# Pairing the PV matmuls behind a score tile in a statically scheduled attention and feed-forward kernel

## The chip, the cores and the metric

The kernel runs on one core of one Trainium2 chip. The metric is the device time of a run in microseconds. Next to the times I use positions read from the traces: when the first projection matmul starts, when the last matmul starts, and where TensorE waits in between.

## The reference, cut to what matters

```python
# x: 2048 tokens x 512; 32 heads of 16; four segments of 512 tokens
for s in range(4):
    logits = einsum(qs, ks) * scale + causal_mask
    a_dot  = einsum(softmax(logits), vs)                    # "score" and "PV"
    a_mem  = (phi(qs) @ M) / (phi(qs) @ z + 1e-6)           # memory numerator, denominator
    o      = sigmoid(beta) * a_mem + (1 - sigmoid(beta)) * a_dot
    M, z   = M + phi(ks).T @ vs, z + phi(ks).sum()
a = o @ wo
h = relu(x @ W_gate) * (x @ W_up);  b = h @ W_down
out = g * a + (1 - g) * b                                   # g = sigmoid(x . gate_w)
```

`phi(t)` is `t + 1` for positive t and `exp(t)` otherwise. On the chip it is an exponential on ACT, then a ramp and a minimum on DVE. TensorE does all the products, ACT the exponentials, POOL the causal mask of the score tiles, and DVE most reads of PSUM.

## The kernel before

The kernel contains a small list scheduler in Python. Every operation is given a planned duration. Before launch the scheduler simulates the five engines and fixes the order on each of them, and the semaphores that keep that order safe. **The order is static.** On the chip nothing is re-decided: if an operation takes longer than planned, whoever was placed behind it waits.

```python
class Sched:
    def _choose(self, e):               # which head of e's queues is placed next
        for q in self.queues[e]:
            ...
            rt = self.ready(op, e)      # planned time at which it could start
            if rt is not None:
                heads.append((q[0], rt, op))          # q[0] is the queue's priority
        ...
        rdy = [h for h in heads if h[1] <= now + 20.0]
        if rdy:
            best = min(rdy, key=lambda h: (h[0], h[1]))
            ...
```

Accumulators use four PSUM banks. A bank is free for a new matmul group when the group that held it has been read by DVE or ACT. Score tiles use the array as four 32-row tiles (mode "r"), PV as four 17-column tiles in 32-column strips (mode "c"), and everything else uses the whole array (mode "f"):

```python
# score tile: 4 heads side by side, one tile per 32 rows
q.matmul(PL[:, jj, o:o + w], lhsT=V.kp[32 * jj:32 * jj + 32, ...], rhs=V.qT[32 * jj:32 * jj + 32, ...],
         start=True, stop=True, tile_position=(32 * jj, 0), ...)
# mask of the diagonal block, on POOL
pool(lambda g, ap=ap: g.affine_select(out=ap, in_=ap, compare_op=ALU.is_ge, fill=0.0, base=0,
                                      pattern=[[0, 4], [1, 128]], channel_multiplier=-1), t_pool(512), ...)
# PV: two operations (p = 0, 1) per group of 8 heads, each with a bank of its own
q.matmul(A(ep)[32 * jj:32 * jj + 17, c:512], lhsT=V.vaug[...], rhs=V.E[:, e, jj, o:o + w],
         start=(j == 0), stop=(j == 3), tile_position=(0, 32 * jj), ...)
# order of one group:  score A0, score B0, [PV pair of the group before], score C, score A1, score B1
```

The argument later turns on two small DVE items. The first is 64 small copies (32 partitions, four gate values in each), which may go to DVE or ACT. In the code they are called `gexpT`. The second is the minimum that finishes phi of the queries, which the denominator matmuls ("den") read:

```python
gq["flex"].append(sc.add(Op([("dve", lambda e, ...: e.tensor_copy(dst, V.gexp[32 * a:32 * a + 32, t0:t1]), 150),   # planned ns
                             ("act", lambda e, ...: e.activation(dst, V.gexp[...], ACT.Copy), 215)], ..., name="gexpT")))
sbs.append(dve(lambda e, G=G: e.tensor_tensor(V.phiq[:, G, :], V.phiq[:, G, :], V.ttmp[:, G % 2, :], ALU.min), t_dve(512, 2), ...))
...
pes.append(pe(fden, 16 * 30, reads=[f"phiq{G}" for G in range(4)] + ["Mbd16"], name=f"den{s}", ep=ep, role="w"))
```

At the start TensorE runs five dummy matmuls until x arrives, transposes x, runs four more dummies, and begins the first projection. The dummies read a tile that DVE zeroes.

The softmax here doesn't subtract the row's maximum and nothing guards it: scores larger than these inputs give would overflow.

Of the kernel before, what the change touches and what calls it, by code (L numbers as in the profile page):

```python
# [13 lines left out]
LAT = 60.0  # L14
# [40 lines left out]

class Op:
    __slots__ = ("engs", "eng", "fns", "occs", "lat", "reads", "writes", "name", "dma", "nbytes", "mode", "ep", "role",
                 "after", "preds", "stream", "idx", "start", "end", "done", "cidx")

    def __init__(self, alts, reads=(), writes=(), name="", lat=0.0, dma=False, nbytes=0, mode="f", ep=None, role=None):  # L60
        self.engs = [a[0] for a in alts]
        self.fns = {a[0]: a[1] for a in alts}
        self.occs = {a[0]: float(a[2]) for a in alts}
        self.eng = self.engs[0] if len(alts) == 1 else None
        self.lat = lat
        self.reads = tuple(reads)
        self.writes = tuple(writes)
        self.name = name
        self.dma = dma
        self.nbytes = nbytes  # L70
        self.mode = mode
        self.ep = ep
        self.role = role
        self.after = 0.0
        self.preds = []
        self.stream = self.idx = self.start = self.end = None
        self.done = False
        if ep is not None:
            if role == "r":
                ep.readers.append(self)  # L80
                self.reads = self.reads + (ep.res,)
            else:
                self.writes = self.writes + (ep.res,)


class Sched:
# [75 lines left out]
    def queue(self, prio, ops):  # L162
# [4 lines left out]
        for e, ts in by.items():  # L167
            self.queues[e].append([prio, ts, 0])

    def _bank_choice(self, op, e):  # L170
        cls = op.ep.cls
        if cls != "att":
            held = 0
            nheld = 0
            for prev in self.bank_ep:
                if prev is None or all(r.done for r in prev.readers):
                    continue
                held += prev.cls == cls
                nheld += 1
            if held >= self.CAPS.get(cls, 2) or nheld >= len(self.bank_ep) - 1:  # L180
                return None
        best = None
        for bi, prev in enumerate(self.bank_ep):
            ft = 0.0
            if prev is not None:
                if not all(r.done for r in prev.readers):
                    continue
                for r in prev.readers:
                    if self.know[e][r.stream] < r.idx:
                        ft = max(ft, r.end + LAT)  # L190
            if best is None or ft < best[1]:
                best = (bi, ft)
        return best
# [7 lines left out]
    def ready(self, op, e):  # L201
        t0 = self.now[e]
        t = op.after
        for p in self._pred_done(op, e):
            if not p.done:
                return None
            if self.know[e][p.stream] < p.idx:
                t = max(t, p.end + LAT)
        if op.ep is not None:
            if op.role == "w" and op.ep.bank is None:  # L210
                for rd in op.ep.readers:
                    for p, _ in rd.preds:
                        if p.ep is op.ep or p.cidx > op.cidx:
                            continue
                        if not p.done:
                            return None
                        t = max(t, p.end - op.occs["pe"] - (3000.0 if op.ep.cls == "out" else 300.0))
                bc = self._bank_choice(op, e)
                if bc is None:
                    return None  # L220
                t = max(t, bc[1])
            elif op.ep.bank is None:
                return None
        if e == "pe" and t > 0:
            t += 80.0
        return max(t, t0)
# [59 lines left out]
    def _choose(self, e):  # L286
        heads = []
        for q in self.queues[e]:
# [4 lines left out]
            op = q[1][q[2]]  # L293
            rt = self.ready(op, e)
            if rt is not None:
                heads.append((q[0], rt, op))
        if not heads:
            return None
        now = self.now[e]
# [81 lines left out]
def program(sc, nc, T, PL, PA, A_x, A_wq, A_wk, A_wv, A_wo, A_beta, W_g, W_u, W_d, gate_w, out, NSEG, KT, NF, NT, EPS, SCALE):  # L381
# [23 lines left out]
    def A(ep):  # L405
        return PA[ep.bank]
# [10 lines left out]
        load(eng, [f"hT{i}"], V.hT[:, i, :], x0[:, i, :], 1 << 17)  # L417
    for nm, w, src in (("wq", V.wq, A_wq), ("wk", V.wk, A_wk), ("wv", V.wv, A_wv)):
        for kt in range(KT):
            load("act" if nm == "wq" and kt % 2 else "sp", [f"{nm}{kt}"], w[:, kt, :], src[kt * 128:(kt + 1) * 128, :], 1 << 17)  # L420
    load("act", ["g4"], V.g4[:], gate_w.rearrange("(kt p) -> kt p", p=128), 1 << 12)
    half = (NF // 2) * 128
    hs_ = ((0, half), (half, NF * 128))
# [46 lines left out]
    sc.queue(1, st)  # L470

    ds = []
    ds.append(dve(lambda e: e.memset(V.rl[:, 0, 0:128], 0.0), 130, writes=["rl0"], name="warm0"))
    for b in range(4):
        ds.append(dve(lambda e, b=b: e.memset(PA[b][:], 0.0), 500, writes=[f"init{b}"], name=f"init{b}"))
    ds.append(dve(lambda e: e.reduce_sum(V.pm[:, :], pm8, AX.X), 180, reads=["pm8"], writes=["pm"], name="pm"))
    sc.queue(0, ds)

    def warm(n, k, b):
        def fn(e):  # L480
            for i in range(n):
                ins = e.matmul(PL[:, b, :], lhsT=V.rl[:, 0, 0:128], rhs=V.rl[:, 0, 0:128].unsqueeze(1).to_broadcast([128, 4, 128]), start=True, stop=True)  # L482
            return ins
        return pe(fn, n * (427 if k == 0 else 260), reads=["rl0"], writes=[f"bankL{b}"], name=f"warm{k}")

    xps, xcs = [warm(5, 0, 3)], []
    for i in range(4):
        def fx(e, i=i):
            for kt in range(KT):
# [6 lines left out]
            xcs.append(dve(lambda e, d=dst, s_=srcp: e.tensor_copy(d, s_), t_dve(512), reads=[f"bankL{i}"], writes=[f"xT0_{i}"], name=f"xc{i}"))  # L496
        else:
            xcs.append(act(lambda e, d=dst, s_=srcp: e.activation(d, s_, ACT.Copy), t_act(512), reads=[f"bankL{i}"], writes=[f"xT0_{i}"], name=f"xc{i}"))
    xps.append(warm(4, 1, 0))
    sc.queue(0, xps)  # L500
    sc.queue(0, [t for t in xcs if t.eng == "dve"])
    sc.queue(0, [t for t in xcs if t.eng == "act"])
# [10 lines left out]
    ep_w = Epoch()  # L513
    gw_pe = pe(lambda e: e.matmul(A(ep_w)[:, 0:KT], lhsT=V.g4[:, :], rhs=V.ident[0:KT, 0:KT], start=True, stop=True), 60, reads=["g4", "ident"], name="gwT", ep=ep_w, role="w")
    gw_act = act(lambda e: e.activation(V.gwc[:], A(ep_w)[:, 0:KT], ACT.Copy), 180, writes=["gwc"], name="gwc", ep=ep_w, role="r")
    gexpT_r = {}
    gq = {"pe": [], "act": [], "dve": [], "flex": [], "sp": []}
    for c in range(NSEG):
# [144 lines left out]

    e_ctr = [0]

    def att(s):
        pes, acts, pools, ds, padd = [], [], [], [], []
        carry = []

        def quad(tag, parts):  # L670
            e = e_ctr[0]
# [18 lines left out]

        def flush():
            if not carry:
                return
            G, eA, eB, eC = carry.pop()
            eps = []
            for p in range(2):
                ep = Epoch("att")
                eps.append(ep)

                def fpv(q, p=p, ep=ep):  # L700
# [3 lines left out]
                            ins = q.matmul(A(ep)[32 * jj:32 * jj + 17, c:512], lhsT=V.vaug[:, s % 2, j, 8 * G + 2 * jj + p, :], rhs=V.E[:, e, jj, o:o + w],  # L704
                                           start=(j == 0), stop=(j == 3), tile_position=(0, 32 * jj), skip_group_check=True)
                    return ins
                pes.append(pe(fpv, mm(1280), reads=[f"E{x}" for x in (eA[p], eB[p], eC)] + [f"E{eA[p]}m0", f"E{eB[p]}m0", f"E{eB[p]}m384", f"E{eC}m{256 * p}"] + va(s), name=f"pv{s}_{G}_{p}", ep=ep, role="w", mode="c"))
            for p in range(2):
                ds.append(dve(lambda e, p=p, ep=eps[p]: e.transpose(V.Tn[:, p, :], A(ep)[:, :]), t_dve(512), writes=[f"Tn{p}"], name=f"tr{s}_{G}_{p}", ep=eps[p], role="r"))  # L709
            Tv = V.Tn[:, :, :].rearrange("q p (c r) -> q p c r", r=32)  # L710
            rv = V.rden[:, :].rearrange("q (p c) -> q p c", p=2)
            gv = V.rdg[:, :].rearrange("q (p c) -> q p c", p=2)
# [7 lines left out]
            else:  # L720
                ds.append(dve(lambda e: e.transpose(V.oTt[:, :], V.adT[:, :]), t_dve(512), reads=["adT"], writes=["oTt"], name=f"bt{s}_{G}"))
                ds.append(dve(lambda e: e.tensor_tensor(V.oT[:, os_, :], V.oTt[:, :], V.amemT[:, G, :], ALU.add), t_dve(512, 2), reads=["oTt"] + [f"amemT{i}" for i in range(4)], writes=[f"oT{os_}"], name=f"oa{s}_{G}"))
        for G in range(4):
            n0, n1 = 2 * G, 2 * G + 1
            eA, eB = [None, None], [None, None]
            eA[0] = quad(f"{G}A0", [(n0, 0, 0, 512)])
            eB[0] = quad(f"{G}B0", [(n0, 1, 0, 384), (n0, 3, 384, 128)])
            flush()
            eC = quad(f"{G}C", [(n0, 2, 0, 256), (n1, 2, 256, 256)])
            eA[1] = quad(f"{G}A1", [(n1, 0, 0, 512)])  # L730
            eB[1] = quad(f"{G}B1", [(n1, 1, 0, 384), (n1, 3, 384, 128)])
            carry.append((G, eA, eB, eC))
        flush()
        return pes, acts, pools, ds

    hctr = [0]
    rctr = [0]
# [65 lines left out]
            tiles = [tiles[0][:-2] + tiles[1][:-2] + tiles[0][-2:-1] + tiles[1][-2:-1] + tiles[0][-1:] + tiles[1][-1:]] + tiles[2:]  # L803
        return [p for g in tiles for p in g], evs, sps

    Q = {k: [] for k in ("patt", "pnd", "pmu", "pproj", "pffn", "pout", "exp", "aphi", "dproj", "dsb", "datt", "dnd", "dmu", "effn", "eout", "pool", "poolmu", "spk", "spa", "spo")}

    def put(**k):
        for n, v in k.items():
            Q[n] += v  # L810
    a, b, c_, d, e_ = proj(0)
    put(pproj=a, dproj=b, dsb=c_, aphi=d, spk=e_)
    for s in range(NSEG):
        if s > 0:
            a, b, c_ = nd(s)
            put(pnd=a, dnd=b, spa=c_)
        a, b, c_, d = att(s)
        put(patt=a, exp=b, pool=c_, datt=d)
        if s < NSEG - 1:
            a, b, c_ = mu(s)  # L820
            put(pmu=a, dmu=b, poolmu=c_)
# [1 line left out]
            put(pproj=a, dproj=b, dsb=c_, aphi=d, spk=e_)  # L823
        a, b, slots = ffn(s)
        put(pffn=a, effn=b)
        a, b, c_ = outp(s, slots)
        put(pout=a, eout=b, spo=c_)
    sc.queue(0, Q["patt"])
    sc.queue(1, Q["pmu"])
    sc.queue(1, Q["pnd"])  # L830
    sc.queue(2, Q["pproj"])
# [64 lines left out]
```

## Time and profile before

| | before |
|---|---|
| median of the first three runs | 274.21 us |
| span of the profiled run | 272.60 us |
| first projection matmul starts / last matmul starts | 6.74 / 269.77 us |
| the stream between the two | 263.03 us |
| visits of score tiles / of PV / mode switches | 80 / 21 / 183 |
| waits of TensorE for DVE in the stream | 0.27 + 0.28 us |

From the page of the before kernel: the span, TensorE's busy time with its share, and the engines' shares of the chain of work that ended last. ("issue" is time in which an engine waited for nothing that the profile shows; DVEq and PEq are the sequencers of DVE and TensorE, PEld is TensorE's loading of weights.)

```profile
span 272.6 us, 5368 instructions
PE 268.2 (98%) x2156; PEld 115.6 (42%) x2156; DVE 206.0 (76%) x421; ACT 192.9 (71%) x182; POOL 123.2 (45%) x171
...
PE 94%; DVE 3%; DMA 1%; ACT 1%; issue 0%; DVEq 0%
```

TensorE is the bound and, for 94% of the span, the critical path. To find what can be saved inside a 98% busy engine, I compared the start of every matmul with the start before it. In one mode, 512-column matmuls follow each other at 0.216 us. A 512-column full-array matmul followed by a score tile takes 0.311 us, and every other change of mode also adds 0.09 to 0.10 us. I use 0.095 us per switch.

The next lines are TensorE's timeline of the before kernel around one group's PV. The columns are the start in us, the duration in us, engine, line, operation, operands and count. L679 is a score tile and L704 is PV.

```profile
67.73 0.40 PE L679 MATMUL psL<-qT,kp 32*128 32x384 bf16 x8
68.05 0.72 PE L704 MATMUL psA<-E,vaug 128*17 128x512 bf16 x16
...
72.26 0.72 PE L704 MATMUL psA<-E,vaug 128*17 128x512 bf16 x16
72.92 0.40 PE L679 MATMUL psL<-qT,kp 32*128 32x512 bf16 x4
```

The two halves of this pair run at different times. Five of the 16 pairs are split like this, so PV has 21 visits instead of 16.

The view of waits for TensorE (before) has three lines. Its idle time counts from the modelled end of the matmul before, so it is a little smaller than the loss read from starts to starts: the third line says 0.2 us where the starts lose 0.274 us.

```profile
PE psL L482 <- DVE rl L473: 1.0, 1, 1.0
PE psL L490 <- DMA hT<-in_A_x_dram: 0.4, 1, 0.4
PE psA L641 <- DVE phiq L592: 0.2, 1, 0.2
```

The third line is the first denominator step, of segment 1, which reads the minimum that finishes phi of the queries. Here is the same place in the before timeline (DVE and PE lines):

```profile
84.28 0.85 DVE L592 TENSOR_TENSOR phiq<-phiq,ttmp 128x512 bf16<-128x512 bf16 x1
84.59 0.40 PE L679 MATMUL psL<-qT,kp 32*128 32x384 bf16 x8
...
85.19 0.59 PE L641 MATMUL psA<-Mbd,phiq 128*128 128x8 bf16 x16 [0.21 <-DVE phiq L592]
```

### The profile page before, as it was taken

The numbers are of one execution on the slowest core, as the hardware profiler recorded it, in microseconds if no ns is written. First come the engines' busy times: TensorE is split into PE (matmuls) and PEld (weight loads), VectorE is DVE, ScalarE is ACT, GpSimd is POOL, SyncE is SP. The second block draws the span as 40 slices with busy tenths as digits, with TensorE's granted clock in tenths as the row PEclk, the third lists the DMA queues.
The fourth block names the chain that finished last, engine by engine and source line by source line (L and its number), as shares of the span: only waits on it lengthen the run. The fifth ranks groups of instructions, "written<-read, shape, count | busy, mean of one in ns | idle before, by whom it ended". The sixth has DMA issues, their size and how long they took to land.

```text
span 272.6 us, 5368 instructions
## 1 busy us (share of the span) xinstructions
PE 268.2 (98%) x2156; PEld 115.6 (42%) x2156; DVE 206.0 (76%) x421; ACT 192.9 (71%) x182; POOL 123.2 (45%) x171
## 2 busy tenths in 40 slices
PE   7999999999999999999999999999999999999996
PEld 4444444344434544344344344344444343434445
DVE  5789989999989998999978949596774256787200
ACT  3279887788696877889578769985866768782122
POOL 4013566629495676847385653242233343331000
PEclk9999999999999999999999999999999999999999
DMA  6999964011001323120112110000111100000011
GB/s 203 332 333 172 290 97 90 13 42 39 20 2 40 79 58 79 38 53 9 22 39 60 38 48 32 19 2 0 25 35 22 38 23 19 0 2 1 0 41 38
DMA packets 31025, 17.01 MB, mean 62 GB/s; under 512 B 20760, under 2 KB 31000, under 8 KB 31000
## 3 DMA queue, kind: packets, MB, share of 16 engines
q1 hardware_dynamic: 30416, 16.14, 23.7%
q10 hardware_dynamic: 584, 0.53, 0.7%
q8 instruction: 17, 0.28, 0.4%
q14 instruction: 8, 0.07, 0.1%
HBM read 9.84 MB, written 2.10 MB: 44 GB/s over the span
## 4 chain that ended last, share of the span: by engine, by line
PE 94%; DVE 3%; DMA 1%; ACT 1%; issue 0%; DVEq 0%
PE psA L749 36%; PE psA L788 18%; PE psA L581 10%; PE psL L679 9%; PE psA L704 7%; PE psA L579 5%; PE psA L781 5%; DMA hT<-in_A_x_dram 1%; PE psA L654 1%; PE psA L625 1%; DVE gexpT L546 1%; PE psL L490 1%; ACT E L684 1%; PE psA L641 1%; DVE hT L760 1%; PE psL L482 0%
## 5 line engine op out<-in xcount | busy, mean ns | idle before, releaser
L684 ACT ACTIVATE E<-psL 128x2048 bf16<-128x2048 f32 x80 | 150.0, 1876 | 39.4 <-PE psL L679 38.8
L687 POOL TENSOR_SCALAR_AFFINE_SELECT E<-E 128x512 bf16<-128x512 bf16 x128 | 83.1, 667 | 116.1 <-ACT E L684 113.0
L749 PE MATMUL psA<-xT,wu 128*128 128x512 bf16 x224 | 59.8, 380 | 0.0
L749 PE MATMUL psA<-xT,wg 128*128 128x512 bf16 x224 | 59.5, 380 | 0.1
L788 PE MATMUL psA<-wd,hT 128*128 128x512 bf16 (+1 forms) x238 | 54.6, 367 | 0.0
L760 DVE TENSOR_TENSOR hT<-psA,rl 128x512 bf16<-128x512 f32 x56 | 38.2, 683 | 14.0 <-PE psA L749 13.1
L788 PEld LDWEIGHTS psA<-wd,hT 128*128 128x128 bf16 x238 | 21.7, 98 | 24.3 <-issue 3.7
L597 POOL TENSOR_SCALAR kp<-kT,pm 128x512 bf16<-128x512 bf16 x19 | 30.7, 1620 | 2.6 <-PE psL L679 1.2
L679 PE MATMUL psL<-qT,kp 32*128 32x384 bf16 (+3 forms) x512 | 31.7, 301 | 0.0
L749 PEld LDWEIGHTS psA<-xT,wu 128*128 128x128 bf16 x224 | 20.4, 98 | 25.4 <-issue 3.1
L749 PEld LDWEIGHTS psA<-xT,wg 128*128 128x128 bf16 x224 | 19.9, 98 | 24.7 <-issue 3.7
L709 DVE STREAM_TRANSPOSE Tn<-psA 128x512 f32<-128x512 f32 x32 | 21.5, 697 | 8.0 <-PE psA L704 7.9
L757 ACT ACTIVATE rl<-psA 128x512 bf16<-128x512 f32 x28 | 16.7, 597 | 12.7 <-PE psA L749 12.5
L679 PEld LDWEIGHTS psL<-qT,kp 32*128 32x128 bf16 x512 | 8.9, 92 | 31.7 <-ACT E L684 14.4
L758 DVE TENSOR_SCALAR rl<-psA 128x512 bf16<-128x512 f32 x28 | 19.0, 680 | 3.6 <-PE psA L749 2.9
L704 PE MATMUL psA<-E,vaug 128*17 128x256 bf16 (+3 forms) x512 | 21.1, 300 | 0.0
L581 PE MATMUL psA<-xT,wq 128*128 128x512 bf16 x64 | 16.5, 380 | 0.0
L781 PE MATMUL psA<-wo,oT 128*128 128x512 bf16 (+1 forms) x68 | 16.5, 367 | 0.0
L581 PE MATMUL psA<-xT,wk 128*128 128x512 bf16 x64 | 16.4, 381 | 0.0
L797 DVE TENSOR_SCALAR osb<-psA,omg 128x512 bf16<-128x512 f32 x8 | 6.0, 746 | 12.9 <-PE psA L788 12.9
L579 PE MATMUL psA<-wv,xT 128*128 128x512 bf16 x64 | 15.7, 380 | 0.0
L798 ACT ACTIVATE osb<-psA,omg 128x512 bf16<-128x512 f32 (+1 forms) x9 | 5.8, 639 | 13.7 <-PE psA L781 13.3
(75 smaller groups left out, 237.1 us busy)
## 6 DMA issues: line engine op xcount, KB each, us to landing
out_dram<-osb SPq DMA_DIRECT2D x15, 128.0 KB, 1.7
wg<-in_B_W_gate_dram SPq DMA_DIRECT2D x8, 224.0 KB, 5.3
wu<-in_B_W_up_dram SPq DMA_DIRECT2D x8, 224.0 KB, 5.8
wd<-in_B_W_down_dram SPq DMA_DIRECT2D x1, 1792.0 KB
osb<-in_A_x_dram SPq DMA_DIRECT2D x12, 128.0 KB, 2.2
wk<-in_A_wk_dram SPq DMA_DIRECT2D x4, 128.0 KB, 4.5
wv<-in_A_wv_dram SPq DMA_DIRECT2D x4, 128.0 KB, 4.0
wo<-in_A_wo_dram SPq DMA_DIRECT2D x1, 512.0 KB, 6.0
```

Source lines behind the costliest of these rows:

```text
L579: ins = e.matmul(A(ep)[:, :], lhsT=V.xT[:, kt, tok + col * 128:tok + (col + 1) * 128], rhs=w[:, kt, :], start=(kt == 0), stop=(kt == KT - 1))
L581: ins = e.matmul(A(ep)[:, :], lhsT=w[:, kt, col * 128:(col + 1) * 128], rhs=V.xT[:, kt, tok:tok + 512], start=(kt == 0), stop=(kt == KT - 1))
L597: km = lambda e, G=G, p=p, ks=ks: e.tensor_scalar(V.kp[:, ks, :], V.kT[:, G, :], V.pm[:, p:p + 1], None, ALU.mult)
L679: ins = q.matmul(PL[:, jj, o:o + w], lhsT=V.kp[32 * jj:32 * jj + 32, kslot(s, n), 128 * j:128 * j + 128], rhs=V.qT[32 * jj:32 * jj + 32, q ...
L684: acts.append(act(lambda a, e=e: a.activation(V.E[:, e, :, :], PL[:, :, :], ACT.Exp, scale=SCALE), t_act(2048), reads=[f"bankL{b}" for b i ...
L687: pools.append(pool(lambda g, ap=ap: g.affine_select(out=ap, in_=ap, compare_op=ALU.is_ge, fill=0.0, base=0, pattern=[[0, 4], [1, 128]], c ...
L704: ins = q.matmul(A(ep)[32 * jj:32 * jj + 17, c:512], lhsT=V.vaug[:, s % 2, j, 8 * G + 2 * jj + p, :], rhs=V.E[:, e, jj, o:o + w], start=(j ...
L709: ds.append(dve(lambda e, p=p, ep=eps[p]: e.transpose(V.Tn[:, p, :], A(ep)[:, :]), t_dve(512), writes=[f"Tn{p}"], name=f"tr{s}_{G}_{p}", e ...
L749: ins = e.matmul(A(ep)[:, :], lhsT=w[:, kt, f * 128:(f + 1) * 128], rhs=V.xT[:, kt, c * 512:(c + 1) * 512], start=(kt == 0), stop=(kt == K ...
L760: evs.append(dve(lambda e, ep=eu, r=r, hs=hs: e.tensor_tensor(V.hT[:, hs, :], A(ep)[:, :], V.rl[:, r, :], ALU.mult), t_dve(512), reads=[f" ...
L781: ins = e.matmul(A(ep)[:, 0:c1 - c0], lhsT=V.oT[:, o0 + G, i * 128:(i + 1) * 128], rhs=V.wo[:, G, c0:c1], start=st_ and G == 0, stop=sp_ a ...
L788: ins = e.matmul(A(ep)[:, 0:c1 - c0], lhsT=V.hT[:, slots[f], i * 128:(i + 1) * 128], rhs=V.wd[:, f, c0:c1], start=st_ and f == f0, stop=sp ...
```

## The change

The intent has four parts.
1. Both PV halves of a group run in one visit directly behind a score tile. The last group of a segment is carried into the next one.
2. When fewer than two banks are free, reads that free a bank get precedence on DVE and ACT.
3. The head gets shorter dummies that read a constant. The queues that load wq are swapped.
4. A tiny gate matmul moves out of the first projection.

The diff, cut to its core (cuts marked with `...`):

```diff
@@ ready @@
+        if op.gate is not None:
+            if self.mode != "r" and not op.gate.done:      # behind a score tile, or once score C is done
+                return None
+            if sum(p is None or all(r.done for r in p.readers) for p in self.bank_ep) < 2:
+                return None                                # a pair needs two free banks
+            t = max(t, ...)
@@ _choose @@
-                heads.append((q[0], rt, op))
+                pr = q[0]
+                if e in ("dve", "act") and op.ep is not None and op.role == "r" and sum(p is None or all(r.done for r in p.readers) for p in self.bank_ep) < 2:
+                    pr = min(pr, 0.5)
+                heads.append((pr, rt, op))
@@ loads @@
-            load("act" if nm == "wq" and kt % 2 else "sp", ...)
+            load("act" if nm == "wq" and kt % 2 == 0 else "sp", ...)
@@ dummies @@
-    xps, xcs = [warm(5, 0, 3)], []          # five of 512 columns; all dummies read a tile that DVE zeroes
+    xps, xcs = [warm(6, 512, 0, 3)], []     # six of 512 columns, reading a constant
 ...
-    xps.append(warm(4, 1, 0))               # four of 512 columns
+    xps.append(warm(8, 128, 1, 0))          # eight of 128 columns
 ...
+    gw_pe.after = 9000.0
@@ att @@
+            pair[0].preds += [d for d in pair[1].preds if d not in pair[0].preds]
+            pvs.extend(pair)                # PV pairs have a queue of their own now
 ...
-            flush()
+            pair = flush()                  # pair of the group before, also across segments
+            if G == 0:
+                between()                   # output of segment s-1 and memory read of s come after it
             eC = quad(...)
+            if pair:
+                pair[0].gate = pes[-1]
...
```

## The prediction

> **What bounds it now.** TensorE. The page's busy table gives PE 98% of the 272.6 us span, and the chain that ended last is 94% PE. In the PE timeline the matmul stream runs without a real hole from 6.7 us to the start of the last matmul at 269.8 us. I compared each matmul's start with the start before it: equal-mode 512-column matmuls follow at 0.216 us. Everything over that pace is in three places.
>
> 1. Mode switches. Score tiles use 32-row tiles, PV 17-column tiles, the rest the full array. A full 512-column matmul followed by a score tile takes 0.311 us instead of 0.216; score to full, score to PV, PV to full cost the same extra, 0.09 to 0.10 us. The Trainium skill ("TensorEngine Tiling (Array Packing)", Key Properties) says changing the mode drains the array; the trace agrees, at about 0.095 us. The timeline has 183 switches (80 score visits, 21 PV visits), about 17.4 us.
> 2. The head, 6.7 us before the first projection: 1.04 us waiting for DVE's memset, five 512-wide dummies at the slow clock, x landing at 3.75 us, transposes to 5.5, four more 512-wide dummies to 6.7.
> 3. Real waits in the stream: about 0.9 us in all, 0.27 and 0.35 us near the two memory-denominator steps (85 and 121 us) and 0.28 us at 129.7 us, where a gate matmul waits for DVE's reading of a bank. The tail after the last matmul (2.8 us: eviction, store) is untouched.
>
> **What the change does.** No matmul of the real work goes away.
> - PV: of 16 pairs, 5 are split into two visits and one or two PV visits stand between full-array matmuls. With every pair in one visit directly behind a score tile there are 16 PV visits; switches fall to 2x80+16 = 176, maybe 177 or 178 if a pair misses its score tile. 7x0.095 = 0.67 us; I take 0.6.
> - Head: the dummies after the transposes shrink from 4x512 to 8x128 columns, from 1.26 us to about 0.85 us at the slow clock. But the first projection also needs the last x copy (ACT, ends 6.32 us) and the first wq block (lands 6.41 us on SP's queue, its ACT twin 6.17 us, which is why the queues are swapped). So it can start near 6.4 instead of 6.74: 0.3 us. The earlier first dummy (no memset wait) gains nothing itself, as x lands at 3.75 anyway. The slow clock ended at about 6 us; the skill ("TensorE: Matmul & The Clock Gate", Part 1) says that window is free-running, so this could move either way by some tenths.
> - Priority for reads that free a bank on DVE and ACT: can only recover the 0.9 us of waits; I take 0.3 us.
> - Carrying the last group delays the previous segment's output projection; feed-forward work fills PE, so nothing lost. The moved little gate matmul (about 0.2 us) costs the same later.
>
> Sum: 1.2 us, nearly all on the critical path, because PE is the path.
>
> **Predicted: 273.0 us**, range 272.2 to 273.9. Faster by over 2%: 0.01; within 2%: 0.985; slower by over 2%: 0.005.
>
> **What would show it.** 16 PV groups of 32 matmuls in the PE timeline, each just behind a score tile; first projection near 6.4 us; the same 0.095 us per switch; last matmul starting about 1.2 us earlier; PE busy still 98%.
>
> **What would make it wrong.** Pairs that miss their slot and stand between full-array matmuls; the two-free-banks condition or the priorities starving the feed-forward of banks, seen as PE waits for DVE or ACT; score tiles delayed so that the last attention group meets the output tiles at the end; a later release of the slow clock.

## The result, and the profile after

Over six runs each, the after kernel's median is 274.13 us and the before kernel's 274.51 us. The ratio is 0.999, with a 95% interval of 0.9977 to 1.0003. (A ratio is the mean time of one kernel's runs over that of the other's of the same rounds, so it is not quite the ratio of the medians.) A second measurement in a later round (run e10 below) gave 0.997 [0.9946, 0.9993]. The two estimates of the gain are 0.1 and 0.3%, by the medians 0.4 and 0.6 us, and the first interval includes no gain at all.

The prediction was 273.0 us with a range of 272.2 to 273.9. It took 1.2 us from the 274.21 us of the first three runs, while the median of six runs of the same before kernel is 274.51 us. So of the 1.1 us between 273.0 and 274.13, 0.3 us is this starting point, and 0.8 us is gain that was forecast and did not come (0.4 us came of 1.2).

The page of the after kernel, same lines:

```profile
span 272.4 us, 5341 instructions
PE 264.6 (97%) x2126; PEld 115.8 (43%) x2161; DVE 206.2 (76%) x411; ACT 196.0 (72%) x194; POOL 120.9 (44%) x168
...
PE 92%; DVE 4%; issue 2%; DMA 1%; ACT 0%
```

This trace lacks 35 matmul records: 2126 matmuls stand against 2161 weight loads. So the 97% does not mean that TensorE became less busy. Each missing record leaves a false hole of about 0.2 us. The views call most of them "issue"; the view of waits puts two of them down to DVE (`PE psA L772 <- DVE gexpT L557` and `PE psA L804 <- DVE oTt L736`, 0.2 us each). I take those holes out by counting the weight loads in them.

TensorE's timeline after (L691 is the score tile, L717 is PV) shows a pair as intended, and one of the two that missed:

```profile
31.01 0.40 PE L691 MATMUL psL<-qT,kp 32*128 32x384 bf16 x8
31.34 1.26 PE L717 MATMUL psA<-E,vaug 128*17 128x512 bf16 x32
...
164.76 0.39 PE L691 MATMUL psL<-qT,kp 32*128 32x512 bf16 x4
165.09 0.61 PE L811 MATMUL psA<-wd,hT 128*128 128x512 bf16 x2
165.62 1.26 PE L717 MATMUL psA<-E,vaug 128*17 128x512 bf16 x32
```

There are 16 PV visits of 32 matmuls. Fourteen stand directly behind a score tile. Two (at 165.6 and 243.4 us) stand between full-array matmuls. That makes 178 switches, five fewer than before.

The new thing is in the view of waits for TensorE (after; two of its eight lines):

```profile
PE psL L492 <- PEq L909: 0.8, 1, 0.8
PE psA L652 <- DVE phiq L603: 0.8, 1, 0.8
...
```

L652 is the denominator step that was L641 before. Its wait grew from 0.274 to 0.957 us, read from starts. Its neighbours in the TensorE timeline after:

```profile
85.09 0.60 PE L811 MATMUL psA<-wd,hT 128*128 128x512 bf16 x2
86.49 0.59 PE L652 MATMUL psA<-Mbd,phiq 128*128 128x8 bf16 x16 [0.79 <-DVE phiq L603]
```

The chain that ended last, in order of time (after; start, us, what), says what it was waiting for:

```profile
83.86 0.16 DVE gexpT L557
84.02 0.03 issue
84.06 0.16 DVE gexpT L557
84.22 0.03 issue
84.25 0.54 DVE gexpT L557
84.79 0.03 issue
84.82 0.56 DVE gexpT L557
...
86.01 0.44 DVE phiq L603
86.44 0.05 issue
86.49 0.59 PE psA L652 x16
```

The critical path leaves TensorE here and runs through seven four-element copies on DVE. Five of them take 0.16 to 0.17 us, and two take 0.54 and 0.56 us. POOL's timeline (after) in the same stretch has two mask instructions:

```profile
84.14 1.23 POOL L699 TENSOR_SCALAR_AFFINE_SELECT E<-E 128x512 bf16<-128x512 bf16 x2 [0.32 <-ACT E L696]
```

By the single records, the masks end at 84.774 and 85.364 us, and the two slow copies end at 84.793 and 85.385 us, 0.02 us after each. The Trainium skill ("SBUF — State Buffer", section "SBUF: two separate sides") says that DVE and GpSimd (POOL) share a port pair, and that it is an exclusive lock: between a GpSimd operation and a DVE operation that runs in a two-port performance mode or has two SBUF inputs, whichever starts first holds it for the whole instruction and the other "fully blocks". The trace does not show the mode of a copy, but its times agree. The five of the 24 DVE copies that took 0.48 to 0.56 us all began while a mask ran and ended about 0.02 us after it. The other 19 took 0.159 to 0.168 us, and two of these began just before a mask.

The account of the stream from the first projection to the last matmul, before to after:

| term | us |
|---|---|
| 5 switches fewer, 5 x 0.095 | -0.48 |
| waits for DVE: before 0.274 + 0.283, after 0.957 + 0.137 | +0.54 |
| first projection at the slow clock in this execution | +0.23 |
| sum / measured (263.03 to 263.29) | +0.29 / +0.26 |

The stream became longer, and the head became shorter by 0.42 us (first projection at 6.32 instead of 6.74 us). Net, the last matmul starts 0.16 us earlier.

### The profile page after: what moved, and what is told of

Its sections match the earlier page's. It is cut to its first block, busy times and chain, and to the rows that moved or that the text cites. A ratio compares the mean times of both kernels' runs of the same rounds, so it can differ in the third digit from the quotient of the medians. Undisturbed runs are those within 1.5% of the kernel's fastest.

```text
span 272.4 us, 5341 instructions
## 1 busy us (share of the span) xinstructions
PE 264.6 (97%) x2126; PEld 115.8 (43%) x2161; DVE 206.2 (76%) x411; ACT 196.0 (72%) x194; POOL 120.9 (44%) x168
## 4 chain that ended last, share of the span: by engine, by line
PE 92%; DVE 4%; issue 2%; DMA 1%; ACT 0%
PE psA L772 36%; PE psA L811 16%; PE psA L592 10%; PE psL L691 9%; PE psA L717 7%; PE psA L590 5%; PE psA L804 4%; DVE gexpT L557 1%; PE psA L665 1%; DMA hT<-in_A_x_dram 1%; PE psA L636 1%; PE psL L500 1%; PE psA L652 1%; DVE qT L599 0%; PE psL L492 0%
## 5 line engine op out<-in xcount | busy, mean ns | idle before, releaser
L772 PE MATMUL psA<-xT,wu 128*128 128x512 bf16 x216 | 58.5, 380 | 0.7 <-issue 0.3
L772 PE MATMUL psA<-xT,wg 128*128 128x512 bf16 x213 | 57.2, 380 | 1.1 <-issue 0.8
L811 PE MATMUL psA<-wd,hT 128*128 128x512 bf16 (+1 forms) x230 | 53.0, 367 | 0.8 <-issue 0.6
L691 PE MATMUL psL<-qT,kp 32*128 32x384 bf16 (+3 forms) x512 | 31.7, 301 | 0.0
L780 ACT ACTIVATE rl<-psA 128x512 bf16<-128x512 f32 x34 | 20.3, 597 | 15.2 <-PE psA L772 11.2
L772 PEld LDWEIGHTS psA<-xT,wg 128*128 128x128 bf16 x224 | 20.2, 98 | 25.0 <-issue 3.1
L772 PEld LDWEIGHTS psA<-xT,wu 128*128 128x128 bf16 x224 | 20.3, 98 | 24.8 <-issue 2.0
L608 POOL TENSOR_SCALAR kp<-kT,pm 128x512 bf16<-128x512 bf16 x16 | 27.3, 1708 | 1.4 <-PE psL L691 0.8
L691 PEld LDWEIGHTS psL<-qT,kp 32*128 32x128 bf16 x512 | 8.9, 92 | 33.5 <-ACT E L696 15.7
L717 PE MATMUL psA<-E,vaug 128*17 128x256 bf16 (+3 forms) x512 | 20.2, 300 | 0.0
L820 DVE TENSOR_SCALAR osb<-psA,omg 128x512 bf16<-128x512 f32 x10 | 7.4, 744 | 14.1 <-PE psA L811 14.1
L781 DVE TENSOR_SCALAR rl<-psA 128x512 bf16<-128x512 f32 x22 | 15.1, 687 | 3.8 <-PE psA L772 3.5
L804 PE MATMUL psA<-wo,oT 128*128 128x512 bf16 (+1 forms) x67 | 16.2, 366 | 0.2 <-DVE oTt L736 0.2
L592 PE MATMUL psA<-xT,wk 128*128 128x512 bf16 x60 | 15.8, 380 | 0.3 <-issue 0.2
L717 PEld LDWEIGHTS psA<-E,vaug 128*17 128x17 bf16 x512 | 10.7, 90 | 9.6 <-issue 2.7
```

The costliest lines, as they stand in the source:

```text
L592: ins = e.matmul(A(ep)[:, :], lhsT=w[:, kt, col * 128:(col + 1) * 128], rhs=V.xT[:, kt, tok:tok + 512], start=(kt == 0), stop=(kt == KT - 1))
L608: km = lambda e, G=G, p=p, ks=ks: e.tensor_scalar(V.kp[:, ks, :], V.kT[:, G, :], V.pm[:, p:p + 1], None, ALU.mult)
L691: ins = q.matmul(PL[:, jj, o:o + w], lhsT=V.kp[32 * jj:32 * jj + 32, kslot(s, n), 128 * j:128 * j + 128], rhs=V.qT[32 * jj:32 * jj + 32, q ...
L717: ins = q.matmul(A(ep)[32 * jj:32 * jj + 17, c:512], lhsT=V.vaug[:, s % 2, j, 8 * G + 2 * jj + p, :], rhs=V.E[:, e, jj, o:o + w], start=(j ...
L772: ins = e.matmul(A(ep)[:, :], lhsT=w[:, kt, f * 128:(f + 1) * 128], rhs=V.xT[:, kt, c * 512:(c + 1) * 512], start=(kt == 0), stop=(kt == K ...
L804: ins = e.matmul(A(ep)[:, 0:c1 - c0], lhsT=V.oT[:, o0 + G, i * 128:(i + 1) * 128], rhs=V.wo[:, G, c0:c1], start=st_ and G == 0, stop=sp_ a ...
```

## The experiments

**Theory.** The terms for switches and for the head are about right, and the saved switches are real. They were given back in a wait of TensorE that the new static order created: den was placed close behind a DVE chain that the plan believed short, and POOL's mask stretches that chain on the chip. **Rivals.** (a) The price of a switch is an artefact of how pipelined matmuls are drawn, so saving switches saves nothing. (b) The new priority pushes phi of the queries back, whatever POOL does. (c) The head's gain is lost later.

This table was worked out from all traces. "Waits" are the losses over 0.03 us where TensorE waited for another engine or a DMA, read from starts after the first projection began. "Slow clock" is the loss in the first projection before the full clock came. Times are medians, with the before kernel of the same rounds beside them.

| run | time / before, us | ratio [95%] | first projection, us | stream, us | switches | waits, us | slow clock, us |
|---|---|---|---|---|---|---|---|
| before | 274.51 | | 6.74 | 263.03 | 183 | 0.56 | 0 |
| after | 274.13 / 274.51 | 0.999 [0.9977, 1.0003] | 6.32 | 263.29 | 178 | 1.09 | 0.23 |
| e1 split pairs | 277.31 / 274.56 | 1.0108 [1.0085, 1.013] | 6.10 | 266.63 | 210 | 0.96 | 0.23 |
| e2 copies' cost in plan | 273.55 / 274.56 | 0.9971 [0.995, 0.9992] | 6.40 | 262.63 | 178 | 0.57 | 0.14 |
| e3 head only | 273.96 / 274.56 | 0.9987 [0.9968, 1.0005] | 6.42 | 263.04 | 183 | 0.56 | 0 |
| e4 priority only | 274.50 / 274.56 | 1.0008 [0.9988, 1.0028] | 6.85 | 263.37 | 181 | 1.11 | 0 |
| e5 short mask, after | 273.01 / 273.90 | 0.9964 [0.9946, 0.9982] | 6.25 | 262.10 | 178 | 0.17 | 0 |
| e6 copies on ACT | 272.85 / 273.90 | 0.9958 [0.9939, 0.9977] | 6.19 | 262.08 | 177 | 0.05 | 0.21 |
| e7 stretch in plan | 272.83 / 273.90 | 0.9963 [0.994, 0.9986] | 6.08 | 261.96 | 177 | 0.16 | 0 |
| e8 no priority | 273.92 / 273.90 | 0.9999 [0.9978, 1.002] | 5.92 | 263.14 | 179 | 1.10 | 0 |
| e9 short mask, before | 273.91 / 274.44 | 0.999 [0.9957, 1.0023] | 6.40 | 262.72 | 183 | 0.29 | 0 |
| e10 after again | 273.83 / 274.44 | 0.997 [0.9946, 0.9993] | 5.96 | 263.05 | 178 | 1.09 | 0 |
| e11 both mends | 272.89 / 274.44 | 0.9947 [0.9913, 0.998] | 6.18 | 262.39 | 177 | 0.58 | 0 |
| e12 copies on ACT, before | 276.19 / 274.44 | 1.0049 [1.0019, 1.0079] | 6.25 | 263.84 | 181 | 1.54 | 0 |

Take the before kernel's stream, add 0.095 us for each switch more and the differences in waits and slow clock, and every row comes out within 0.1 us of its measured stream. (For e1, add also the 16 inserted matmuls at 0.025 us.) In the last round of four (e9 to e12), single executions of several kernels were 1.5 us or so longer at the same clock: two of the 11 before runs took 275.81 us. What made them longer is not known. So those intervals are wide, and for these four I rest on the traces, of one execution each. The rounds also differ among themselves (the before kernel's medians run from 273.90 to 274.56 us), so a time is compared with the before kernel of its own round.

### e1: double the disputed cost

```diff
 def fpv(q, p=p, ep=ep):
+    if p == 1:      # overwritten by the next matmul
+        q.matmul(A(ep)[:, 0:1], lhsT=V.E[:, eA[p], 0, 0:128], rhs=V.E[:, eA[p], 0, 0:1], start=True, stop=True)
     src = [...]
```

> The after kernel with one 1-column full-array matmul put between the two halves of each of the 16 PV pairs: 32 more mode switches, 16 more tiny matmuls, the same order otherwise (the tiny result is overwritten by the next matmul). Theory (a switch really costs TensorE about 0.095 us and TensorE is the path): 32 x 0.095 + 16 x 0.025 = +3.4 us over the after kernel, about 277.5 us, and the last matmul starts 3.4 us later. Rival (the cost per switch is only how the trace draws pipelined matmuls, and saving it saves no time): at most +0.6 us.

Measured: 277.31 us, and the stream is 3.34 us longer than in the after kernel (266.63 against 263.29). TensorE's timeline of e1:

```profile
31.12 0.72 PE L719 MATMUL psA<-E,vaug 128*17 128x512 bf16 x16
31.78 0.18 PE L715 MATMUL psA<-E 128*128 128x1 bf16 x1
31.89 0.72 PE L719 MATMUL psA<-E,vaug 128*17 128x512 bf16 x16
```

Sixteen such interruptions cost 3.34 us net, or 0.21 us each for two switches and a one-column matmul (the 0.137 us wait of the after kernel is not in this run). This rules out rival (a): switches cost what they seem to cost. The wait at den is there again (0.959 us).

### e2: tell the plan the copies' real cost

```diff
-... e.tensor_copy(dst, V.gexp[32 * a:32 * a + 32, t0:t1]), 150),
+... e.tensor_copy(dst, V.gexp[32 * a:32 * a + 32, t0:t1]), 280),
```

> The after kernel, but the static scheduler is told 280 ns instead of 150 ns for each of the small gate copies on DVE (the trace shows 0.195 us apart, some 0.55 us). Theory (the gain was eaten by the 0.96 us that TensorE waits for DVE's phiq before the first memory-denominator step, and that wait comes from the copies being planned too short): the wait falls under 0.2 us, the switches stay at 178, the time falls by about 0.8 us to 273.3 us. Rival (the wait belongs to the new priorities, which push phiq back whatever the plan says, or it shows up elsewhere): waits over 0.7 us in all remain and the time stays within 0.3 us of the after kernel.

Measured: 273.55 us, 0.58 us under the after kernel's median (274.13, of another round; the stream is 0.66 us shorter). The den wait is gone. The expected 0.8 us was missed because a new wait stands elsewhere in the new order, as the waits of e2 show:

```profile
PE psA L592 <- DVE Tn L722: 0.4, 1, 0.4
```

By starts it is 0.574 us at 112.0 us: a projection matmul needs the bank that DVE's transpose of a PV result has yet to read. Just before it, DVE's phi operations took 0.85 us where the plan has 0.42. So lateness of the same size in DVE's work moved the wait to another place.

### e3: the head alone

```diff
-    xps, xcs = [warm(5, 0, 3)], []
+    xps, xcs = [warm(6, 512, 0, 3)], []
...   (eight dummies of 128 columns, queues of wq swapped, little gate matmul later; nothing else)
```

> The before kernel with only the change of the head: dummies from a constant, 6x512 and 8x128, wq queues swapped, the little gate matmul later. Prediction on record: -0.3 us (274.2). Reading of the after trace: the first projection starts 0.42 us sooner but may still meet the slow clock, which gives back up to 0.25 us: -0.2 us. Rival: the head gain is lost later, 0.0 us. Switches 183 as before.

Measured: ratio 0.9987, interval 0.9968 to 1.0005. The trace is clearer than the clock: the first projection starts 0.32 us sooner, and the stream is 263.04 us against 263.03. In these two executions the head's gain is kept to the end, which speaks against rival (c). The start itself varies between executions: over all 14 traces it lies between 6.25 and 6.85 us with the old head (four traces, mean 6.56) and between 5.92 and 6.42 us with the new one (ten, mean 6.18). In this execution the full clock came early (3.93 us), and the projection then waited for a wq block instead:

```profile
PE psA L581 <- DMA wq<-in_A_wq_dram: 0.9, 1, 0.9
```

### e4: the priority alone

```diff
-                heads.append((q[0], rt, op))
+                pr = q[0]
+                if e in ("dve", "act") and op.ep is not None and op.role == "r" and ... < 2:
+                    pr = min(pr, 0.5)
+                heads.append((pr, rt, op))
```

> The before kernel with only the new priority for bank-releasing reads on DVE and ACT. If the priorities are what delays phiq (rival), the first memory-denominator step waits about 0.9 us here too, and the time is 0.3 us over before or more. If not (theory), its wait stays near 0.27 us, the 0.28 us wait at the gate matmul near 130 us goes, switches fall from 183 to 181, and the time falls by about 0.4 us to 274.1 us.

Measured: no gain (1.0008), and neither side was fully right. The den wait stays at 0.281 us, so the priority alone does not delay phi there. Two switches fewer, and the wait at 130 us is gone, as the theory said. But three new waits for DVE appear between 120 and 123 us, 0.83 us together (0.208, 0.174 and 0.450 us). Two lines of e4's view of waits:

```profile
PE psA L584 <- DVE Tn L712: 0.3, 1, 0.3
PE psA L644 <- DVE phiq L595: 0.2, 1, 0.2
```

### e5: take POOL out of DVE's way, same order

```diff
-pools.append(pool(lambda g, ap=ap: g.affine_select(out=ap, ..., pattern=[[0, 4], [1, 128]], ...), t_pool(512), ...))
+apx = V.E[:, e, :, o:o + 2]
+pools.append(pool(lambda g, ap=apx: g.affine_select(out=ap, ..., pattern=[[0, 4], [1, 2]], ...), t_pool(512), ...))
```

The planned durations are untouched, so every engine has exactly the after kernel's order.

> The after kernel, same order on every engine, but POOL's causal mask works on 2 of 128 columns (the result is wrong on purpose). Theory (the 0.96 us wait before the first memory-denominator step comes from DVE standing still while POOL's mask instruction runs: two of the small gate copies took 0.55 us instead of 0.16 us): the copies all take 0.16 to 0.17 us, the wait falls to 0.1 to 0.3 us, the time falls by about 0.8 us to 273.3 us. Rival (DVE is late simply because its queue holds too much work before phiq, POOL has no part in it): copies stay over 0.4 us in places, the wait stays over 0.8 us.

Measured: 273.01 us. The DVE copies, by the view of their source line (durations are min/median/max in ns), in the after kernel:

```profile
L557 DVE COPY gexpT<-gexp x24: 159/165/561, 26.2 to 173.5; 32x4 f32<-32x4 f32 x24
```

and in e5:

```profile
L557 DVE COPY gexpT<-gexp x24: 159/164/199, 25.1 to 171.8; 32x4 f32<-32x4 f32 x24
```

The timeline of e5 around the first denominator:

```profile
83.58 1.33 DVE L557 COPY gexpT<-gexp 32x4 f32<-32x4 f32 x7
...
83.85 0.37 POOL L700 TENSOR_SCALAR_AFFINE_SELECT E<-E 128x8 bf16<-128x8 bf16 x2 [0.32 <-ACT E L696]
...
84.94 0.42 DVE L603 TENSOR_TENSOR phiq<-phiq,ttmp 128x512 bf16<-128x512 bf16 x1
...
85.42 0.59 PE L652 MATMUL psA<-Mbd,phiq 128*128 128x8 bf16 x16
```

The seven copies take 1.33 us instead of 2.11 us. The wait falls from 0.957 to 0.174 us, and the second one (0.137 us) goes too. The time happens to be the predicted 273.0 us, but that is luck in part: the before kernel of this round took 273.90 us, so the gain is 0.89 us and not 1.2, and the short mask helps the before kernel as well (e9). The order is the same (the two traces have the same sequences of weight loads and of instructions on DVE, ACT and POOL) and only the mask is shorter, so this settles the cause: DVE stood still behind POOL's mask, and TensorE stood still behind DVE.

The two-input DVE operations show the same. In the after trace the phi-of-queries minimum took 0.42 us on average with no POOL instruction beside it, and 0.70 us beside a mask. Of the six beside a mask, the four that began while the mask ran took 0.82 to 0.87 us, and the two that began before it took 0.42 us.

### e6 and e7: two mends

In e6 the copies leave DVE:

```diff
-gq["flex"].append(sc.add(Op([("dve", ...tensor_copy..., 150), ("act", ...activation..., 215)], ...
+gq["flex"].append(sc.add(Op([("act", ...activation..., 215)], ...
```

> The after kernel with all 64 small gate copies on ACT, none on DVE (24 were on DVE). The static plan then has 177 switches and no hole. Theory: the first denominator's wait falls under 0.3 us; if no new wait of DVE appears elsewhere the stream from first projection to last matmul is 262.3 us, and the time 273.1 us. Rival (ACT's 24 more copies delay score tiles' exponentials or bank reads, new waits over 0.5 us): within 0.3 us of the after kernel.

In e7 the plan is told the stretched durations:

```diff
-e.tensor_copy(dst, V.gexp[...]), 150)          +280
-phi minimum, output add:  t_dve(512, 2)        +560
-phi ramp:                 t_dve(512, 4)        +380
```

> The after kernel with the static scheduler told the measured mean times of the DVE operations that POOL stretches: gate copies 280 ns (150), phi minimum and output add 560 ns (422), phi ramp 380 ns (288). 177 switches planned. Theory: with the late DVE work known to the plan, waits of TensorE for DVE in the stream fall under 0.4 us in all (1.09 us in the after kernel), time about 273.1 us. Rival: every new order has new waits of the same size; time 273.6 us or more.

Measured: 272.85 and 272.83 us, with ratios of 0.9958 and 0.9963 to before. Both beat the before kernel of their own round, and both results are correct. The after kernel did not run in that round; against it the streams are 1.0 to 1.3 us shorter. In each of the two, the view of TensorE's waits has a single line left, the first dummy's (the 0.05 and 0.16 us of the table are losses from starts to starts that this view does not list). The line of e7:

```profile
PE psL L492 <- PEq L909: 0.8, 1, 0.8
```

Both have 177 switches and streams of 262.08 and 261.96 us. They also reorder everything, so the exact size of their gain contains luck of the order. The same-order run e5 is the proof of the cause, and these two show that the gain can be had in a correct kernel.

### e8: the after kernel without the priority

```diff
-                pr = q[0]
-                if e in ("dve", "act") and ...: pr = min(pr, 0.5)
-                heads.append((pr, rt, op))
+                heads.append((q[0], rt, op))
```

> The after kernel without the new priority of bank-releasing reads. The plan has 179 switches and two holes of about 0.48 us where a matmul waits for a bank near 107 and 113 us. Theory (the priority is needed with the pairs, since a pair takes two banks at once, but it is not what made the first denominator wait): about 0.9 us over the after kernel, 275.0 us, with waits on banks near 107 and 113 us. Rival (the priority caused the wait): the time falls by 0.5 us or more under the after kernel.

Measured: ratio 0.9999 to before, with a stream of 263.14 us, hardly different from the after kernel's 263.29 and 263.05. It is neither 0.9 us slower nor 0.5 us faster. The 0.957 us wait is gone in this order, but four others add up to 1.10 us. Two of them in e8's view of waits:

```profile
PE psA L589 <- DVE Tn L719: 0.4, 1, 0.4
PE psA L801 <- ACT osb L818: 0.2, 1, 0.2
```

So the priority plays a part in where the wait stands, but taking it away does not mend anything. Rival (b) explains one place and not the sum.

### e9: the short mask in the before kernel, same order

The edit is that of e5.

> The before kernel, same order, with POOL's mask on 2 of 128 columns (wrong result on purpose): the partner of the short-mask run of the after kernel. Theory: its waits of 0.27 us (first denominator) and 0.28 us (gate matmul near 130 us) mostly go, so the stream from first projection to last matmul falls from 263.03 us to 262.5 us or a little more, against 262.10 us in the after kernel with short masks: with POOL out of the way the change is worth its switches (5 x 0.095 = 0.48 us less) in the stream. Time about 273.7 us. Rival (the change is worth nothing even then): stream 262.1 us.

Measured: the den wait goes, the 0.285 us wait at 129 us stays, and the stream is 262.72 us. Against e5's 262.10 us the whole change is worth 0.62 us in the stream once POOL's stretch is out of the way: 0.48 us of switches and 0.11 us of waits (0.285 against 0.174). The wait at 129 us did not "mostly go", so it is a hole of the plan itself. The plan itself leaves 0.41 us before that matmul.

### e10: the after kernel again

> The after kernel unchanged, for a second measurement beside the others: 0.1% faster than before, within 0.3%; the wait before the first denominator is again 0.95 to 0.97 us; only the head (landing of x, moment of the full clock) may differ.

Measured: 273.83 against 274.44 us. The waits are 0.949 and 0.137 us, in the same two places, so they belong to the order and not to one execution. Here the first projection met the full clock and started at 5.96 us.

### e11: both mends

The edits are e6's plus planned 480 ns (phi minimum), 520 ns (output add) and 330 ns (phi ramp).

> The after kernel with both mends: all small gate copies on ACT, and the plan told 480 ns (phi minimum), 520 ns (output add), 330 ns (phi ramp). 177 switches planned, no hole. Theory: waits of TensorE in the stream under 0.3 us, as in the runs with one mend each; time 0.4% under before; hardly better than one mend alone, as only about 0.2 us of waits is left to take. Rival: another order, a new wait over 0.5 us.

Measured: 272.89 us, ratio 0.9947. It is not better than one mend. A new 0.583 us wait stands at 13.8 us, where the first score tile needs a masked key from DVE:

```profile
PE psL L690 <- DVE kp L607: 0.5, 1, 0.5
```

The rival came true here: another order, another wait.

### e12: the copies' mend on the before kernel

The edit is e6's, on the before kernel.

> The before kernel with only the small gate copies moved to ACT (32 were on DVE). Question: does this mend alone, without the paired PV and the priority, give the gain? The plan has 181 switches and holes of 0.38, 0.31 and 0.22 us, where a matmul waits for a bank or an exponential. Theory: no: the stream stays between 262.7 and 263.5 us, time within 0.2% of before. Rival (the copies were the whole matter): 0.4% faster as with the after kernel.

Measured: the stream is 263.84 us, longer than the theory allowed, with six waits of 0.05 to 0.59 us, among them 0.269 us for a DMA at 33.8 us. The profiled run took 274.64 us and is the fastest of six. The median is 276.19 us, and no trace shows what made the other five longer. So the copies were not "the whole matter". Moving them helped with the after kernel's rules and cost here.

## Why the prediction was wrong, point by point

- **"TensorE" is the bound; a switch costs about 0.095 us.** Right. In e1, 32 switches and 16 one-column matmuls cost 3.34 us.
- **"switches fall to 2x80+16 = 176, maybe 177 or 178"; "I take 0.6".** Nearly right: 178 switches, 0.48 us.
- **Head, "0.3 us".** About right in size. In the after kernel's profile the gain was 0.42 us, and 0.23 us of it was given back at the slow clock. In e3 it was 0.32 us with nothing given back. The prediction named the clock as a term that moves by some tenths: in these traces the full clock, where recorded, came anywhere from 3.50 to 6.80 us.
- **"Real waits in the stream: about 0.9 us in all".** A misreading. There were 0.274 and 0.283 us. The trace has no loss over 0.03 us near 121 us. The "0.35 us" was a sum over the 10 us from 120 us on, and it contained the 0.283 us at 129.7 us. I counted it twice.
- **"can only recover the 0.9 us of waits; I take 0.3 us".** This is the step that failed. The waits went from 0.56 to 1.09 us, so a term of -0.3 was +0.54 us. The prediction let the new rules act on the old waits only ("can only recover"), as if the rest of the order stayed. It does not: pairs and priority re-draw the whole static order once, from planned durations, and whether that order has waits on the chip is decided by the operations that take longer than planned. The new order left den little slack behind seven copies and the phi minimum. In the planned times (both schedulers run on a CPU), 0.48 us lie between the end of that minimum and the start of den before the change, and 0.14 us after it. The copies were planned at 0.15 us each (1.05 us). They took 2.11 us, 0.78 us of it because of POOL's mask (e5). With the mask short, the same order waits 0.174 us there instead of 0.957. In the plan the stream became 0.98 us shorter (261.90 to 260.92 us), so on paper the gain was there; on the chip the stream became 0.26 us longer.
- **"What would make it wrong" named the missed pairs and the waits for DVE.** The first happened twice. Of the second the sign came, a wait of TensorE for DVE, but not in the way named: den waited for its operand, and not the feed-forward part for a bank. The profile already showed the stretch: in the before trace the same copies take 164 ns at the median and 589 ns at the most. I did not look at the spread.

What stays open: whether the new priority is worth keeping under a truthful plan. With the untruthful one it is worth nothing either way (e4, e8). The faster kernels e6 and e7 were only run with it. Which part of the change, pairs or priority, took den's slack is not separated either: the long wait is absent with the priority alone (e4) and without it (e8), and there only with both.

## What to carry to other kernels

When the order is fixed before launch, a change of priority or pairing is a new draw of the whole order. Its gain has to be weighed against the waits that planned-too-short operations will open somewhere else. So compare planned with measured durations first, and look at the maximum and not only the median, above all for DVE operations that share a port with POOL. To test a suspected delay, shorten the suspect while every order stays the same (e5): in a static schedule an edit of rules or planned durations moves everything.

## What the Trainium skill lacked or had wrong

- "TensorEngine Tiling (Array Packing)", Key Properties, says a change of tiling mode drains the array but gives no price. Here it is about 0.095 us per switch, whichever two of the three modes: 183 switches cost 17.4 us of 272.6 us, an estimate from that price.
- "SBUF — State Buffer", sections "SBUF: two separate sides" and "Who interferes with whom": nothing wrong was found, and copies are named there among the operations that can contend. What these sections lack is a number for a very small one: a copy of four fp32 elements in each of 32 partitions went from 0.16 us to 0.48 to 0.56 us, ending 0.02 us after POOL's mask.
- "GPSIMD Engine Reference", section "Key points", puts DVE at about 2x GpSimd for elementwise work. For multiplying a 128x512 bf16 tile by a per-partition scalar, the after trace has a median of 345 ns on DVE and 1584 ns on POOL, 4.6x (POOL's spans in a profile are rough). The plan had 680 ns for POOL.
- "TensorE: Matmul & The Clock Gate", Part 1, says the activity window is free-running. The traces agree: full clock at 3.50 to 6.80 us in the 11 traces that recorded it, of kernels whose dummies all started by 1.04 us.
- No page says that matmul records can be missing: five of the 14 traces lacked 35 or 36, each leaving a hole of 0.2 us that looks like a wait.
